# Wider recurrence operations, paired gate products, layer norm on ScalarE and a new order inside `y`, in a fused state-space and SwiGLU kernel

## The chip, the cores and the metric

The kernel runs on one core of one Trainium2 chip. The metric is the device time of one execution in microseconds (us). TensorE (PE) multiplies matrices into PSUM; VectorE (DVE), ScalarE (ACT) and GpSimd (POOL) do the rest; SyncE (SP) issues most DMAs. Each engine works through its own instructions in program order.

## The reference

Two branches read the same layer-normed input and are added to it. `x` is 2048 x 512, the state has 512 complex elements, F is 1792; everything is in bf16 outside.

```
xn = layernorm(x)                                   # over the 512 features, no weights
# branch A: diagonal complex state space model
dt = exp(log_dt); Lam_bar = exp(dt * Lam)
B_bar = ((Lam_bar - 1) / Lam)[:, None] * Bmat
Bu = einsum("bld,pd->blp", xn, B_bar)
for t in range(L): h = Lam_bar * h + Bu[:, t]       # complex
yA = 2 * real(einsum("blp,dp->bld", hseq, Cmat)) + xn * Dskip
# branch B: SwiGLU
yB = (silu(xn @ w1) * (xn @ w3)) @ w2
out = x + yA + yB
```

## The kernel before

The 2048 rows are cut into four blocks of 512 (`b`), each of four chunks of 128 (`cl`). Features, states and F are cut into tiles of 128: 4 feature tiles (`dt`), 4 state tiles (`pt`), 14 F tiles (`f`).

- **Layer norm.** `ln_first` does block 0: statistics and apply on VectorE, transposes on TensorE, copies of PSUM into `xnT` on ScalarE. `ln_tasks(b)` makes the tasks of the other blocks: `ln_stats` of a chunk on VectorE, `finish_stats` on POOL, `apply` on VectorE with a DMA transpose of `xn` into `xnT` on SP's queue.
- **Parameters.** `params` and `params_w` make from `log_dt` and `Lambda` the decay `rho`, the angle per step `turn` and the complex weight `w2c`, on 128 x 4 elements, mostly on POOL. `table_angles(pt)` makes the cosines and sines `tabe` of 512 steps (four VectorE operations, three sines on ScalarE), `table_q(pt)` multiplies them by `w2c` into `tabq`.
- **`glu(b)`.** For each `f` eight matmuls of 512 columns into two PSUM tiles `gu_ps` (of four), then `evac`: `Silu` of one and a copy of the other on ScalarE (`g16`, `u16`); `gate` multiplies them on VectorE into `hgT`.
- **`bu(b)`.** For each state tile the real and imaginary input, four matmuls each into `bu_ps`, copied by ScalarE into `u`.
- **The recurrence** (`ssm_tasks`). The rotation by the angle tables turns the complex recurrence into two real ones. Per state tile: `pre` rotates `u` (three VectorE operations on 128 x 1024), two `scan` of 512 steps with decay `rho`, `post` rotates back into `h` (three operations). The scan of block b starts from the last column of `h` of block b − 1.
- **`res_tasks(b)`.** `xn * Dskip + x`, two VectorE operations on 128 x 2048.
- **`y(b)`.** For each chunk 14 matmuls of `hgT` with `w2` and 8 of `h` with `ct_re` and `ct_im` into one PSUM tile `y_ps` (of two); `finish` adds the residual on VectorE and sends the chunk out by DMA on SP's queue.

The order of the work on VectorE is set by a queue of tasks, `Filler`: each task has a cost in us, and the code of `glu`, `bu` and `y` calls `bg.fill(budget)` after a group of matmuls. A fill issues tasks while half the cost of the next one is within the budget carried so far; `flush(key)` issues all up to the last one with that key. In `y` before the change:

```
            if cl == CPB - 1 and b == NBLK - 1:
                bg.fill(100.0)
            else:
                bg.fill(4.0)
            while len(pend) > 1:
                finish()
```

The order of the whole is glu(0), bu(0), glu(1), bu(1), y(0), glu(2), bu(2), y(1), bu(3), glu(3), y(2), y(3). DMA loads stand in SP's queue in the order written, `late_loads` (blocks 2 and 3 of `x`, `dskip_row`, `ct_re`, `ct_im`) as the last task of the first queue.

Of the kernel before, what the change touches and what calls it, by code (L numbers as in the profile page):

```python
# [21 lines left out]
class Filler:  # L22
# [8 lines left out]

    def fill(self, budget):
        self.debt += budget
        while self.tasks and self.tasks[0][0] * 0.5 <= self.debt:
            cost, fn, _ = self.tasks.popleft()
            self.debt -= cost
            fn()
        if not self.tasks:
            self.debt = min(self.debt, 0.0)

    def flush(self, key):
        last = -1
        for i, t in enumerate(self.tasks):
            if t[2] == key:
                last = i
# [8 lines left out]
def kernel(  # L54
# [133 lines left out]
    def ln_first():  # L188
        ln_alloc(0)
        for h in range(2):  # L190
            c0 = 2 * h
            for cl in (c0, c0 + 1):
                ln_stats(0, cl)
            lnv = lnp.tile([P, 2], FP32, name="lnv")
            nc.scalar.activation(out=lnv, in_=mv_all[:, c0:c0 + 2, 1], func=ACT.Ln, bias=eps_t, scale=1.0)
            nc.scalar.activation(out=rstd_all[:, c0:c0 + 2], in_=lnv, func=ACT.Exp, scale=-0.5)
            for cl in (c0, c0 + 1):
                ln_apply(0, cl)
                pxt = ps_y.tile([P, NDT, P], BF16, name="y_ps")
                for dt in range(NDT):  # L200
                    nc.tensor.transpose(out=pxt[:, dt, :], in_=xn_blk[0][:, cl, dt * P:(dt + 1) * P], identity=ident)  # L201
                nc.scalar.activation(out=xnT_blk[0][:, :, cl * P:(cl + 1) * P], in_=pxt, func=ACT.Copy)

    def ln_tasks(b):
# [100 lines left out]
    def bu(b):  # L305
        for pt in range(NPT):
            u = up.tile([P, 2, TBLK], BF16, name="u")
            for ri, bt in ((0, bt_re), (1, bt_im)):
                ps = ps_bu.tile([P, TBLK], FP32, name="bu_ps")
                for dt in range(NDT):  # L310
                    nc.tensor.matmul(out=ps, lhsT=bt[:, dt, pt * P:(pt + 1) * P], rhs=xnT_blk[b][:, dt, :],  # L311
# [211 lines left out]
```

## Time and profile before

| | |
|---|---|
| time, median of 3 runs | 236.75 us (236.69 to 237.62) |
| the profiled execution | 236.88 us, span 234.7 us |
| mean granted TensorE clock | 0.975 |
| TensorE matmuls busy | 210.3 us (90% of the span) |
| VectorE busy | 173.9 us (74%) |
| ScalarE busy | 97.1 us (41%) |

The span runs from the first to the last instruction of the profiled execution. Matmuls are pipelined and their ends are modelled, so TensorE's busy time is not time at its peak; the granted clock is 1.00 at 2.4 GHz.

### The profile page before, as it was taken

What the parts mean: (1) busy time and instruction counts of PE and PEld (TensorE: products, weight loads), DVE (VectorE), ACT (ScalarE), POOL (GpSimd) and SP (SyncE); (2) the same over time, 40 slices, a digit from 0 to 9 for tenths busy, and PEclk for the clock granted to TensorE, in tenths of its full rate; (3) what the DMA queues carried; (4) which work ended last, traced back from release to release, by engine and by line L of the source; (5) the groups of instructions that cost most, each with busy time, mean ns of one, the idle gap of its engine ahead of it and who ended that gap; (6) DMA issues with size and microseconds to landing.
All of it is one profiled execution on the core that took longest, in us unless ns stands there. A gap on an engine that the chain in (4) does not pass through costs nothing.

```text
span 234.7 us, 2666 instructions
## 1 busy us (share of the span) xinstructions
PE 210.3 (90%) x942; PEld 96.0 (41%) x961; DVE 173.9 (74%) x293; ACT 97.1 (41%) x171; POOL 14.5 (6%) x46
## 2 busy tenths in 40 slices
PE   0689989929999999599999999699999999999993
PEld 0454434314444444244444444244444444444441
DVE  2509799992989797996899599996999989711111
ACT  3459978614676630003676650002766670000000
POOL 6046002000000002000000100000000000000000
PEclk9999999997999999799999999889999999999998
DMA  6999500159300002201000031001000000100010
GB/s 191 353 303 253 199 3 0 22 128 216 106 0 0 0 3 45 67 22 45 0 3 3 0 67 22 25 22 45 0 0 3 0 0 0 46 24 22 22 45 24
DMA packets 25596, 13.66 MB, mean 58 GB/s; under 512 B 15472, under 2 KB 25584, under 8 KB 25584
## 3 DMA queue, kind: packets, MB, share of 16 engines
q1 hardware_dynamic: 25200, 13.24, 20.8%
q10 hardware_dynamic: 288, 0.26, 0.3%
q8 instruction: 7, 0.11, 0.2%
q14 instruction: 5, 0.04, 0.1%
q0 software_dynamic: 96, 0.00, 0.0%
HBM read 7.74 MB, written 2.10 MB: 42 GB/s over the span
## 4 chain that ended last, share of the span: by engine, by line
PE 62%; DVE 27%; ACT 2%; DMA 2%; issue 2%; POOL 2%; POOLq 0%; SPq 0%; ACTq 0%
PE gu_ps L363 33%; PE y_ps L428 17%; PE y_ps L431 9%; DVE g L335 4%; DVE stats L176 3%; PE bu_ps L311 3%; DVE hgT L375 2%; DVE xn L181 2%; DVE tabq L293 1%; DVE tabq L298 1%; DVE v L329 1%; DVE ang L282 1%; DMA x_blk<-in_A_x_dram 1%; DMA xnT<-xn 1%; DVE mv_all L177 1%
## 5 line engine op out<-in xcount | busy, mean ns | idle before, releaser
L363 PE MATMUL gu_ps<-xnT,w_sb 128*128 128x512 bf16 (+1 forms) x456 | 101.7, 383 | 6.8 <-DMA xnT<-xn 4.5
L363 PEld LDWEIGHTS <-w_sb 128*128 128x128 bf16 x464 | 46.6, 101 | 60.7 <-issue 10.1
L428 PE MATMUL y_ps<-w_sb,hgT 128*128 128x512 bf16 x219 | 53.9, 398 | 4.9 <-DVE o L421 4.6
L428 PEld LDWEIGHTS <-hgT 128*128 128x128 bf16 x224 | 22.7, 102 | 34.0 <-issue 9.7
L313 ACT ACTIVATE u<-bu_ps 128x512 bf16<-128x512 f32 x32 | 19.0, 597 | 31.1 <-PE bu_ps L311 31.1
L421 DVE TENSOR_TENSOR o<-y_ps,xn 128x512 bf16<-128x512 f32 x16 | 11.0, 685 | 27.5 <-PE y_ps L431 24.2
L335 DVE TENSOR_TENSOR_SCAN g<-rho,h,v 128x512 bf16<-128x512 f32 x24 | 30.0, 1274 | 0.2
L431 PEld LDWEIGHTS <-h 128*128 128x128 bf16 x128 | 12.5, 98 | 15.1
L311 PE MATMUL bu_ps<-xnT,bt_re 128*128 128x512 bf16 x62 | 16.2, 379 | 0.6 <-ACT u L313 0.5
L431 PE MATMUL y_ps<-ct_re,h 128*128 128x512 bf16 x63 | 16.4, 379 | 0.1
L311 PE MATMUL bu_ps<-xnT,bt_im 128*128 128x512 bf16 x62 | 16.3, 379 | 0.2
L431 PE MATMUL y_ps<-ct_im,h 128*128 128x512 bf16 x63 | 16.2, 379 | 0.0
L176 DVE BATCH_NORM_STATS2 stats<-x_blk 128x6 f32<-128x512 bf16 x16 | 10.8, 676 | 3.4 <-DMA x_blk<-in_A_x_dram 3.4
L368 ACT ACTIVATE g_1102<-gu_ps 128x512 bf16<-128x512 f32 x1 | 0.6, 598 | 23.7 <-PE gu_ps L363 23.7
L311 PEld LDWEIGHTS <-bt_re 128*128 128x128 bf16 x64 | 6.3, 98 | 8.3 <-issue 0.9
L335 DVE TENSOR_TENSOR_SCAN g<-rho,v 128x512 bf16<-128x512 f32 x8 | 9.5, 1212 | 0.0
L201 PE MATMUL y_ps<-ident,xn 128*128 128x128 bf16 x16 | 2.1, 308 | 8.2 <-DVE xn L181 8.2
L311 PEld LDWEIGHTS <-bt_im 128*128 128x128 bf16 x64 | 6.3, 98 | 7.5
L181 DVE TENSOR_SCALAR xn<-x_blk,mv_all,rstd_all 128x512 bf16<-128x512 bf16 x16 | 5.6, 408 | 4.2 <-POOL rstd_all L210 2.9
L209 POOL TENSOR_SCALAR vpe<-mv_all 128x4 f32<-128x4 f32 x3 | 0.8, 255 | 107.5 <-DVE mv_all L177 107.5
L260 DVE RECIPROCAL sc<-sc 128x4 f32<-128x4 f32 x1 | 0.2, 179 | 8.1 <-POOL sc L255 8.1
L201 PEld LDWEIGHTS <-xn 128*128 128x128 bf16 x16 | 1.5, 135 | 8.4 <-DVE xn L181 8.4
(331 smaller groups left out, 215.5 us busy)
## 6 DMA issues: line engine op xcount, KB each, us to landing
w_sb<-in_B_w_dram SPq DMA_DIRECT2D x6, 512.0 KB, 8.2
out_dram<-o SPq DMA_DIRECT2D x16, 128.0 KB, 1.7
w_sb<-in_B_w_dram SPq DMA_DIRECT2D x1, 1792.0 KB, 10.2
x_blk<-in_A_x_dram SPq DMA_DIRECT2D x3, 512.0 KB, 4.2
w_sb<-in_B_w_dram SPq DMA_DIRECT2D x2, 256.0 KB, 4.4
x_blk<-in_A_x_dram ACTq DMA_DIRECT2D x2, 128.0 KB, 3.0
x_blk<-in_A_x_dram SPq DMA_DIRECT2D x2, 128.0 KB, 2.7
xnT<-xn SPq DMA_TRANSPOSE x12, 2.4
```

Source lines behind the costliest of these rows:

```text
L176: nc.vector.bn_stats(out=stats, in_=x_blk[b][:, cl, :])
L177: nc.vector.bn_aggr(out=mv_all[:, b * CPB + cl, :], in_=stats)
L181: nc.vector.tensor_scalar(out=xn_blk[b][:, cl, :], in0=x_blk[b][:, cl, :], scalar1=mv_all[:, c, 0:1], scalar2=rstd_all[:, c:c + 1], op0=AL ...
L201: nc.tensor.transpose(out=pxt[:, dt, :], in_=xn_blk[0][:, cl, dt * P:(dt + 1) * P], identity=ident)
L311: nc.tensor.matmul(out=ps, lhsT=bt[:, dt, pt * P:(pt + 1) * P], rhs=xnT_blk[b][:, dt, :], start=(dt == 0), stop=(dt == NDT - 1))
L313: nc.scalar.activation(out=u[:, ri, :], in_=ps, func=ACT.Copy)
L335: nc.vector.tensor_tensor_scan(out=st["g", pt][:, ri, :], data0=rho[:, pt:pt + 1].to_broadcast([P, TBLK]), data1=st["v", pt][:, ri, :], in ...
L363: nc.tensor.matmul(out=ps[:, tsl], lhsT=w[:, dt, f * P:(f + 1) * P], rhs=xnT[:, dt, tsl], start=(dt == 0), stop=(dt == NDT - 1))
L375: nc.vector.tensor_tensor(out=hgT[:, f, :], in0=g16, in1=u16, op=ALU.mult)
L421: nc.vector.tensor_tensor(out=o, in0=y_ps, in1=xn_blk[b][:, cl, :], op=ALU.add)
L428: nc.tensor.matmul(out=y_ps, lhsT=hg_blk[b][:, f, tsl], rhs=w2_sb[:, f, :], start=(f == 0), stop=False)
L431: nc.tensor.matmul(out=y_ps, lhsT=h_blk[b][:, pt, ri, tsl], rhs=ct[:, pt, :], start=False, stop=(ri == 1 and pt == NPT - 1))
```

## The change

- Filler: only tidied (`pop`).
- Block 0's layer norm is split: `ln_first_pair` (statistics and apply of two chunks) and `ln_first_transpose`. The half-width matmuls of the first two `f` are issued after the first pair, and the second pair's transposes between the two halves. The transpose of the parameters stands ahead of the first matmuls, in a `bu_ps` tile; the table load for `Silu` stands after the last copy into `xnT`. The third `f` takes its PSUM from `ps_bu`.
- The first queue has a new order; `late_loads` is issued after `glu(0)`.
- `ln_scalar_engine(b)`, for blocks 2 and 3, replaces their tasks: sum by `Copy`, sum of squares by `Square`, apply by `Identity`, all on ScalarE, with the small steps on POOL. It is issued just ahead of `y(0)` and `y(1)`.
- The recurrence takes two state tiles in each operation (128 x 2048), and writes over its inputs: over `u` before and in the scans, over `h` after them. Its operations are tasks of their own.
- Gate products are made for two `f` at once (128 x 1024).
- `y` issues the gate part of two chunks, then the state part of each with its `finish`.
- Buffers: `glup` 3 to 2 (of double size), `up` 6 to 3 (of double size), `outp` 3 to 2.

```diff
-    glup = ctx.enter_context(tc.tile_pool(name="glup", bufs=3))
+    glup = ctx.enter_context(tc.tile_pool(name="glup", bufs=2))
...
-    up = ctx.enter_context(tc.tile_pool(name="up", bufs=6))
+    up = ctx.enter_context(tc.tile_pool(name="up", bufs=3))
...
+    def ln_scalar_engine(b):
+
+        ln_alloc(b)
+        acc = lnp.tile([P, 4, CPB], FP32, name="acc")
+        sm, nm, ss, nb = (acc[:, i, :] for i in range(4))
+        rstd = rstd_all[:, b * CPB:(b + 1) * CPB]
+        xn, gp = xn_blk[b], nc.gpsimd
+        for cl in range(CPB):
+            nc.scalar.activation(out=xn[:, cl, :], in_=x_blk[b][:, cl, :], func=ACT.Copy, accum_out=sm[:, cl:cl + 1])
+        gp.tensor_scalar(out=nm, in0=sm, scalar1=-1.0 / D, scalar2=None, op0=ALU.mult)
+        for cl in range(CPB):
+            nc.scalar.activation(out=xn[:, cl, :], in_=x_blk[b][:, cl, :], func=ACT.Square, bias=nm[:, cl:cl + 1],
+                                 scale=1.0, accum_out=ss[:, cl:cl + 1])
+        gp.tensor_scalar(out=ss, in0=ss, scalar1=1.0 / D, scalar2=LN_EPS, op0=ALU.mult, op1=ALU.add)
+        gp.tensor_tensor(out=rstd, in0=ss, in1=mhalf, op=ALU.pow)
+        gp.tensor_tensor(out=nb, in0=nm, in1=rstd, op=ALU.mult)
+        for cl in range(CPB):
+            nc.scalar.activation(out=xn[:, cl, :], in_=x_blk[b][:, cl, :], func=ACT.Identity,
+                                 bias=nb[:, cl:cl + 1], scale=rstd[:, cl:cl + 1])
+            ln_transpose(b, cl)
...
+    def params(pps, between):
         nc.scalar.activation(out=par, in_=pps, func=ACT.Copy)
         nc.scalar.activation(out=dtv, in_=par[:, 0:NPT], func=ACT.Exp)
         gp.tensor_tensor(out=kr, in0=dtv, in1=lre, op=ALU.mult)
+        between()
...
+        for hf in range(NPT // 2):
+            u = up.tile([P, 2, 2, TBLK], BF16, name="u")
+            u_blk[b, hf] = u
+            for j in range(2):
+                pt = 2 * hf + j
...
+            bg.fill(3.4)
...
+        FULL = [P, 2, 2, TBLK]
+
+        def half(hf):
+            psl = slice(2 * hf, 2 * hf + 2)
+            st = {}
+
+            def pre_a():
+                if hf == 0:
+                    h_blk[b] = hp.tile([P, NPT, 2, TBLK], BF16, name="h")
+                st["g"] = u_blk[b, hf]
+                st["p"] = ssmw.tile(FULL, BF16, name="p")
+                nc.vector.tensor_tensor(out=st["p"], in0=st["g"], in1=tabq[:, psl, 2:3, :].to_broadcast(FULL),
+                                        op=ALU.mult)
+
+            def pre_b():
+                nc.vector.tensor_tensor(out=st["g"], in0=st["g"], in1=tabq[:, psl, 0:2, :], op=ALU.mult)
+
+            def pre_c():
+                nc.vector.tensor_tensor(out=st["g"], in0=st["g"], in1=st["p"][:, :, ::-1, :], op=ALU.subtract)
+
+            def scan(j, ri):
+                pt = 2 * hf + j
+                init = 0.0 if b == 0 else h_blk[b - 1][:, pt, ri, TBLK - 1:TBLK]
+                v = st["g"][:, j, ri, :]
+                nc.vector.tensor_tensor_scan(out=v, data0=rho[:, pt:pt + 1].to_broadcast([P, TBLK]), data1=v,
+                                             initial=init, op0=ALU.mult, op1=ALU.add)
+
+            def post_a():
+                st["p"] = ssmw.tile(FULL, BF16, name="p")
+                nc.vector.tensor_tensor(out=st["p"], in0=st["g"], in1=tabe[:, psl, 1:3, :], op=ALU.mult)
+
+            def post_b():
+                nc.vector.tensor_tensor(out=h_blk[b][:, psl, :, :], in0=st["g"],
+                                        in1=tabe[:, psl, 0:1, :].to_broadcast(FULL), op=ALU.mult)
+
+            def post_c():
+                nc.vector.tensor_tensor(out=h_blk[b][:, psl, :, :], in0=h_blk[b][:, psl, :, :],
+                                        in1=st["p"][:, :, ::-1, :], op=ALU.subtract)
+
+            for fn in (pre_a, pre_b, pre_c):
+                bg.add(1.2, fn)
+            for j in range(2):
+                for ri in range(2):
+                    bg.add(1.25, lambda j=j, ri=ri: scan(j, ri))
+            for fn in (post_a, post_b, post_c):
+                bg.add(1.2, fn, ("ssm", b))
...
+            if f % 2 == 0:
+                pair[:] = [glup.tile([P, 2, TBLK], BF16, name="g16"), glup.tile([P, 2, TBLK], BF16, name="u16")]
+            g16, u16 = pair
+            nc.scalar.activation(out=g16[:, f % 2, :], in_=g_ps, func=ACT.Silu)
+            nc.scalar.activation(out=u16[:, f % 2, :], in_=u_ps, func=ACT.Copy)
+            if f % 2 == 1:
+                pend.append((f, g16, u16))
...
+                evs = [ln_first_transpose(2 * hf + i) for i in range(2)]
+                if hf == 0:
+                    pps = params_transpose()
+                    for ev in evs:
+                        ev()
+                    ln_first_pair(1)
+                else:
+                    params(pps, evs[0])
+                    evs[1]()
+                    nc.scalar.preload_act_table_set("silu_and_others")
...
+            bg.fill(4.0)
+            gate()
         for f in range(f0, NFT):
-            g_ps = ps_gu.tile([P, TBLK], FP32, name="gu_ps")
+            pool, name = (ps_bu, "bu_ps") if b == 0 and f == f0 else (ps_gu, "gu_ps")
+            g_ps = pool.tile([P, TBLK], FP32, name=name)
             mms(g_ps, w1_sb, f, slice(0, TBLK))
-            u_ps = ps_gu.tile([P, TBLK], FP32, name="gu_ps")
+            u_ps = pool.tile([P, TBLK], FP32, name=name)
             mms(u_ps, w3_sb, f, slice(0, TBLK))
             evac(f, g_ps, u_ps)
-            bg.fill(1.3)
-            while len(pend) > 1:
+            bg.fill(1.35)
+            if pend and f % 2 == 0:
...
+        tiles = {}
+
+        def from_gate(cl):
+            tiles[cl] = ps_y.tile([P, D], FP32, name="y_ps")
             for f in range(NFT):
-                nc.tensor.matmul(out=y_ps, lhsT=hg_blk[b][:, f, tsl], rhs=w2_sb[:, f, :], start=(f == 0), stop=False)
+                nc.tensor.matmul(out=tiles[cl], lhsT=hg_blk[b][:, f, cl * P:(cl + 1) * P], rhs=w2_sb[:, f, :],
+                                 start=(f == 0), stop=False)
+
+        def from_state(cl):
             for ri, ct in ((0, ct_re), (1, ct_im)):
                 for pt in range(NPT):
-                    nc.tensor.matmul(out=y_ps, lhsT=h_blk[b][:, pt, ri, tsl], rhs=ct[:, pt, :],
+                    nc.tensor.matmul(out=tiles[cl], lhsT=h_blk[b][:, pt, ri, cl * P:(cl + 1) * P], rhs=ct[:, pt, :],
                                      start=False, stop=(ri == 1 and pt == NPT - 1))
-            pend.append((cl, y_ps))
-            if cl == CPB - 1 and b == NBLK - 1:
-                bg.fill(100.0)
-            else:
-                bg.fill(4.0)
-            while len(pend) > 1:
-                finish()
-        return finish
-
-
-    ln_first()
-    ln1a, ln1b = ln_tasks(1)
+
+        def finish(cl):
+            o = outp.tile([P, D], BF16, name="o")
+            nc.vector.tensor_tensor(out=o, in0=tiles[cl], in1=xn_blk[b][:, cl, :], op=ALU.add)
+            nc.sync.dma_start(out=ov[:, b * CPB + cl, :], in_=o)
+
+        for cl in range(0, CPB, 2):
+            from_gate(cl)
+            bg.fill(2.8)
+            from_gate(cl + 1)
+            bg.fill(2.8)
+            if cl == 0:
+                bg.flush(("ssm", b))
+                bg.flush(("res", b))
+            from_state(cl)
+            finish(cl)
+            bg.fill(1.0)
+            from_state(cl + 1)
+            finish(cl + 1)
+            bg.fill(1.0)
...
+    bg.add(1.9, lambda: table_angles(0))
     bg.add(0.2, params_w)
-    for i in range(NPT + 1):
-        if i < NPT:
-            bg.add(1.9, lambda pt=i: table_angles(pt))
-        for t in ln1a[i:i + 1]:
-            bg.add(*t)
-        if i >= 1:
-            bg.add(2.1, lambda pt=i - 1: table_q(pt))
+    ln1a, ln1b = ln_tasks_vector(1)
+    for t in ln1a:
+        bg.add(*t)
+    bg.add(1.9, lambda: table_angles(1))
+    bg.add(2.4, lambda: table_q(0))
     for t in ln1b:
         bg.add(*t, ("ln", 1))
-    bg.add(0.0, late_loads)
+    for i in range(2, NPT):
+        bg.add(1.9, lambda pt=i: table_angles(pt))
+        bg.add(2.4, lambda pt=i - 1: table_q(pt))
+    bg.add(2.4, lambda: table_q(NPT - 1))
...
+    late_loads()
...
+    ln_scalar_engine(2)
+    y(0)
...
+    ln_scalar_engine(3)
+    y(1)
```

## Rows read from the trace of the kernel before

**Rows 1.** The page: busy time of engines, and ScalarE's in 40 slices (tenths).

```profile
PE 210.3 (90%) x942; PEld 96.0 (41%) x961; DVE 173.9 (74%) x293; ACT 97.1 (41%) x171; POOL 14.5 (6%) x46
...
ACT  3459978614676630003676650002766670000000
```

**Rows 2.** TensorE timeline: start, us, instruction and count, idle time before it.

```profile
10.03 3.62 PE L363 MATMUL gu_ps<-xnT,w_sb 128*128 128x256 bf16 x16
...
16.70 9.01 PE L363 MATMUL gu_ps<-xnT,w_sb 128*128 128x512 bf16 x39 [0.57 <-ACT g_259 L368]
...
45.91 1.03 PE L311 MATMUL bu_ps<-xnT,bt_im 128*128 128x512 bf16 x4
51.46 26.02 PE L363 MATMUL gu_ps<-xnT,w_sb 128*128 128x512 bf16 x110 [4.52 <-DMA xnT<-xn]
...
84.22 3.19 PE L428 MATMUL y_ps<-w_sb,hgT 128*128 128x512 bf16 x14
...
107.62 24.34 PE L363 MATMUL gu_ps<-xnT,w_sb 128*128 128x512 bf16 x110
131.79 1.03 PE L311 MATMUL bu_ps<-xnT,bt_re 128*128 128x512 bf16 x4
...
138.70 3.19 PE L428 MATMUL y_ps<-w_sb,hgT 128*128 128x512 bf16 x14
...
161.57 1.03 PE L311 MATMUL bu_ps<-xnT,bt_re 128*128 128x512 bf16 x4
...
192.69 3.18 PE L428 MATMUL y_ps<-w_sb,hgT 128*128 128x512 bf16 x14
...
229.89 1.03 PE L431 MATMUL y_ps<-ct_im,h 128*128 128x512 bf16 x4
```

**Rows 3.** Windows of 5 us: busy time of each engine, PEclk, DMA share, GB/s.

```profile
50.00:55.00 5.00, 3.54 (x11) 1.42 (x12) 2.59 (x5) 1.19 (x2) 0.00 (x0) 0.73 0.76 181
```

**Rows 4.** Waits: who waited for whom, us in total, times, longest.

```profile
PE y_ps L428 <- DVE o L421: 4.6, 2, 2.6
```

**Rows 5.** VectorE timeline.

```profile
17.57 0.18 DVE L260 RECIPROCAL sc<-sc 128x4 f32<-128x4 f32 x1 [8.10 <-POOL sc L255]
...
44.54 1.38 DVE L181 TENSOR_SCALAR xn<-x_blk,mv_all,rstd_all 128x512 bf16<-128x512 bf16 x4
...
95.72 0.67 DVE L421 TENSOR_TENSOR o<-y_ps,xn 128x512 bf16<-128x512 f32 x1
...
138.74 2.46 DVE L335 TENSOR_TENSOR_SCAN g<-rho,h,v 128x512 bf16<-128x512 f32 x2
...
145.22 2.46 DVE L335 TENSOR_TENSOR_SCAN g<-rho,h,v 128x512 bf16<-128x512 f32 x2
```

**Rows 6.** DMA issues: KB each, median us from issue to landing.

```profile
xnT<-xn SPq DMA_TRANSPOSE x12, 2.4
...
par_rows<-in_A_Lambda_im_dram POOLq DMA_DIRECT2D x1, 1.0 KB, 3.5
```

**Rows 7.** Groups by line: count, busy us, mean ns of one, idle before.

```profile
L335 DVE TENSOR_TENSOR_SCAN g<-rho,h,v 128x512 bf16<-128x512 f32 x24 | 30.0, 1274 | 0.2
...
L404 DVE TENSOR_TENSOR xn<-xn,dskip_row 128x2048 bf16<-128x2048 bf16 x4 | 4.9, 1218 | 0.0
L210 POOL TENSOR_TENSOR rstd_all<-vpe,mhalf 128x4 f32<-128x4 f32 x3 | 3.1, 1035 | 0.2
L293 DVE SCALAR_TENSOR_TENSOR tabq<-tabe,w2c,tq 128x512 bf16<-128x512 bf16 x4 | 3.0, 752 | 0.1
...
L285 ACT ACTIVATE tabe<-rnd,halfpi 128x512 bf16<-128x512 f32 x4 | 2.9, 722 | 2.0 <-DVE rnd L283 2.0
...
L243 ACT ACT_TABLE_LOAD x1 | 1.3, 1283 | 0.0
...
L325 DVE TENSOR_TENSOR p_599<-u,tabq 128x1024 bf16<-128x1024 bf16 x1 | 0.7, 685 | 0.0
```

**Rows 8.** ScalarE timeline at the front.

```profile
6.90 1.09 ACT L202 ACTIVATE xnT<-y_ps 128x512 bf16<-128x512 bf16 x2 [1.15 <-PE y_ps L201]
```

More of the change, by code (lines that the diff above doesn't have):

```diff
@@ L30, in add, with pop @@
         self.tasks.append((cost, fn, key))
+    def pop(self):
+        cost, fn, _ = self.tasks.popleft()
+        self.debt -= cost
+        fn()
     def fill(self, budget):
@@ L34, in fill @@
         while self.tasks and self.tasks[0][0] * 0.5 <= self.debt:
-            cost, fn, _ = self.tasks.popleft()
-            self.debt -= cost
-            fn()
+            self.pop()
         if not self.tasks:
@@ L41, in flush @@
     def flush(self, key):
[L42 to L45, printed above, removed]
+        last = max((i for i, t in enumerate(self.tasks) if t[2] == key), default=-1)
         for _ in range(last + 1):
-            cost, fn, _ = self.tasks.popleft()
-            self.debt -= cost
-            fn()
+            self.pop()
         self.debt = max(self.debt, -4.0)
@@ L186, in ln_alloc, with ln_first_pair, ln_first_transpose, ln_transpose @@
         xnT_blk[b] = xtp.tile([P, NDT, TBLK], BF16, name="xnT")
[L188 to L204, printed above, removed]
+    def ln_first_pair(h):
+        c0 = 2 * h
+        for cl in (c0, c0 + 1):
+            ln_stats(0, cl)
+        lnv = lnp.tile([P, 2], FP32, name="lnv")
+        nc.scalar.activation(out=lnv, in_=mv_all[:, c0:c0 + 2, 1], func=ACT.Ln, bias=eps_t, scale=1.0)
+        nc.scalar.activation(out=rstd_all[:, c0:c0 + 2], in_=lnv, func=ACT.Exp, scale=-0.5)
+        for cl in (c0, c0 + 1):
+            ln_apply(0, cl)
+    def ln_first_transpose(cl):
+        pxt = ps_y.tile([P, NDT, P], BF16, name="y_ps")
+        for dt in range(NDT):
+            nc.tensor.transpose(out=pxt[:, dt, :], in_=xn_blk[0][:, cl, dt * P:(dt + 1) * P], identity=ident)
+        return lambda: nc.scalar.activation(out=xnT_blk[0][:, :, cl * P:(cl + 1) * P], in_=pxt, func=ACT.Copy)
+    def ln_transpose(b, cl):
+        nc.sync.dma_start_transpose(out=xnT_blk[b][:, :, cl * P:(cl + 1) * P], in_=xn_blk[b][:, cl, :])
+    def ln_tasks_vector(b):
         csl = slice(b * CPB, (b + 1) * CPB)
@@ L305, in bu @@
     def bu(b):
[L306 to L311, printed above, removed]
-                                     start=(dt == 0), stop=(dt == NDT - 1))
-                nc.scalar.activation(out=u[:, ri, :], in_=ps, func=ACT.Copy)
-            u_blk[b, pt] = u
-            bg.fill(1.7)
@@ new lines, in bu @@
+        for hf in range(NPT // 2):
[3 more added lines that the diff above has]
+                pt = 2 * hf + j
+                for ri, bt in ((0, bt_re), (1, bt_im)):
+                    ps = ps_bu.tile([P, TBLK], FP32, name="bu_ps")
+                    for dt in range(NDT):
+                        nc.tensor.matmul(out=ps, lhsT=bt[:, dt, pt * P:(pt + 1) * P], rhs=xnT_blk[b][:, dt, :],
+                                         start=(dt == 0), stop=(dt == NDT - 1))
+                    nc.scalar.activation(out=u[:, j, ri, :], in_=ps, func=ACT.Copy)
+            bg.fill(3.4)
@@ new lines, in ssm_tasks @@
+    def ssm_tasks(b):
+        FULL = [P, 2, 2, TBLK]
[35 more added lines that the diff above has]
+                bg.add(1.2, fn, ("ssm", b))
+        for hf in range(NPT // 2):
+            half(hf)
```

89 lines of the change are left out of this document (15 added, 74 removed).

## The prediction

> **What bounds the kernel now.** I read the page first. TensorE (PE) is busy 90% of the span, VectorE (DVE) 74% [rows 1]. So the end is set by the matmuls, plus whatever keeps them from running back to back at the full clock.
>
> Next I read the TensorE timeline, which shows where that happens [rows 2]. Two stretches are clean. From 107.62 one `glu` takes until 131.79 (24.17 us, 1.73 a step of two tiles) and one `bu` until 138.70 (6.91 us), 31.08 together. The last two calls of `y` run from 192.69 to 229.89 + 1.03 = 230.92, 19.12 us each; a tile has 22 matmuls, so its 14 of the gate take 3.03 us and its 8 of the state 1.74. Against these, four stretches are too long.
> - Ahead of `glu(1)` TensorE stands still from 45.91 + 1.03 = 46.94 to 51.46 (4.52 us), waiting for the DMA transposes of block 1's layer norm. The `glu` and `bu` behind it take 84.22 − 51.46 = 32.76 us, 1.68 too many. The windows show why: 50 to 55 ran at a granted clock of 0.73 [rows 3], that is, partly at 1.2 GHz instead of 2.4 after the standstill. Two more windows, in `y(0)` and `y(1)`, look like it.
> - `y(0)` takes 107.62 − 84.22 = 23.40 us, 4.28 too many, and `y(1)` 161.57 − 138.70 = 22.87 us, 3.75 too many. The list of waits holds the cause: twice a tile of `y_ps` waits for `o` on VectorE, 2.6 us and 2.0 [rows 4]; the rest is again the slower clock after it.
> - The front: the half-width matmuls begin at 10.03, the full-width ones at 16.70 after waiting 0.57 us for ScalarE, and `bu(0)` ends at 46.94 [rows 2].
>
> All other time is matmuls at their pace, and 3.8 us from the last matmul to the end of the span.
>
> The VectorE timeline names what is late [rows 5]. Block 1's layer norm is applied only at 44.54, because the filler queue has all angle tables and `tabq` tables ahead of it. VectorE itself idled until 17.57, for the parameter chain on POOL. In `y(0)`, `finish` of tile 0 starts at 95.72, though its tile, the first of the four, was complete at 84.22 + 4.8 = 89.0: it stands behind queued recurrence work.
>
> **The change part by part.** I make the sum against the profiled execution, 236.88 us (span 234.7 and 2.18 around it); the median of the runs shown is 236.75.
>
> *Layer norm of block 1 earlier.* In the new queue its statistics follow `table_angles(0)` and its four applies follow `table_q(0)`. By the filler's bookkeeping (1.35 a step against the tasks' costs) the applies are issued in steps f = 6 and 7 of `glu(0)`, about 27 us into the span; a transpose lands 2.4 us after its issue [rows 6], so near 31. They are needed near 45. The standstill and its slow clock go: −4.52 − 1.68 = −6.2. `late_loads` still stands behind these transposes on SP's queue; its `ct_re` and `ct_im` are wanted only in `y(0)`, near 80.
>
> *The order inside `y`.* `from_gate` of two tiles comes first, then the state part of each, with its `finish` at once. The third tile needs the buffer that `finish` of tile 0 frees. That `finish` can start when the first state part is done, 2 × 3.03 + 1.74 = 7.8 us into `y`; TensorE asks for the buffer at 9.5. What counts is how much VectorE has queued ahead of that `finish`. For `y(0)`, counted from the start of `bu(1)`: the last gate product and three tasks, then from 5.4 on half of block 1's recurrence through its scans, to about 14.1; the state part ends at 6.9 + 7.8 = 14.7. No wait. For `y(1)`, counted from `bu(2)`: the recurrence can't start before the first pair of `u` is evacuated at 4.1, and a whole half (12.1 us, below) stands ahead of `finish`, which ends at 16.2 + 0.7 = 16.9; TensorE asks at 16.4. A wait of 0.5 us. For `y(2)`: tasks until 7.8, just in time. So −4.3 for `y(0)` and −3.75 + 0.5 = −3.2 for `y(1)`.
>
> *Recurrence two tiles wide, in place.* A row like the new operations exists: `xn` times the broadcast `dskip_row`, 2048 wide and written over its input, 1.22 us [rows 7]. So neither width, nor writing over an input, nor a broadcast costs the rate. A 1024-wide product takes 0.685. A state tile took 145.22 − 138.74 = 6.48 us from scans to scans [rows 5], two of them 12.96. A half block is now six wide operations and four scans; consecutive operations overlap by some 0.03 (two scans of 1.274 took 2.46 with what follows), so 6 × 1.2 + 4 × 1.23 = 12.1 us. The scan with its output over its input has no row: not less than the row of 1.274 [rows 7], for it does the same steps, and at most twice that; I take the row, for only an address differs. Gate products in pairs: by the slope of the two rows one of 512 takes 0.42, so 28 × (2 × 0.42 − 0.685) is some 4 us. So VectorE loses 8 × 0.86 = 7 and 4 us, and besides these the layer norm of blocks 2 and 3 (the applies alone 1.38 a block [rows 5]). The end sees none of it directly, since VectorE is not waited for outside the places above; it is the slack on which they rest. Were it to cost as much as before, `y(1)` would wait 0.7 us longer.
>
> *Layer norm of blocks 2 and 3 on ScalarE.* Per block twelve activations 512 wide, four small POOL operations (the power takes 1.04 [rows 7]) and four transposes. They start as `y` starts, where ScalarE has nothing else (the zeros in its slices [rows 1]). The forms that accumulate a sum have no row. Below: 0.5 us, from two copies in 1.09 [rows 8]; above: twice the sine with a bias, 0.72 [rows 7], in case a second instruction reads the sum. I take 0.75, as that sine too has an operand per partition: 12 × 0.75 + 2.2 (POOL) + 0.6 + 2.4 (last transpose) + 0.3 = 14.5 us, against the 19.1 of `y`. Cost 0; at the upper price it is 22.8, and the reader of `xnT` would wait 3.7. The Trainium skill, "ScalarE: Activation LUTs", section "What ACT_TABLE_LOAD costs", gives 186 ns plus 0.833 ns an element, 93 ns more for each per-partition operand, and 93 ns of overlap; by it the twelve would take an estimated 7.3 us instead of 9, and the sum would stay. No run here has timed these forms yet.
>
> *The front.* The first-half matmuls need only the first two chunks of `xnT`, ready at 6.90 + 1.09 = 7.99 [rows 8], not the 10.03 of before. `par_rows`, now read just ahead of them, lands 3.5 after an issue among the first of the span [rows 6], in time. Sixteen take 3.55, to 11.6; but now the second pair's transposes and ScalarE copies (about 1.0 each) stand between the halves, and the second half starts at 13.5, hardly earlier than it did. The table load (1.28) runs beside it, so the 0.57 wait goes: full-width matmuls from about 15.6, against 16.70. From there to the end of `bu(0)` the work is 12 × 1.73 + 6.91 = 27.7 us; before it took 46.94 − 16.70 = 30.2. Two waits stay. In step 3 VectorE has a gate product, two statistics and four angle operations to do, until about 21, and the three sines behind them hold up ScalarE's evacuations: about 1.0 us on TensorE. The last angle table does the same to `bu(0)`, 0.5. So `bu(0)` ends at 15.6 + 27.7 + 1.5 = 44.8: −2.1. Bounds: no gain (46.9), and no wait at all (15.3 + 27.7 = 43.0, −3.9).
>
> **Sum:** −6.2 − 4.3 − 3.2 − 2.1 = −15.8, so 236.88 − 15.8 = 221.1 us; the span near 219.
>
> **Rivals.**
> *A. `finish` is late again.* If each wide operation costs 0.15 us more than I take, the eight or nine ahead of `finish` make it 1.3 us later: `y(1)` waits 1.8, `y(0)` about 0.7. After waits of 2.0 and 2.6 the clock fell, and took another 1.7 each time. Price 2 to 7 us: 223 to 228. For it: margins of 0.6 and −0.5. Against: the row at 1.22.
> *B. ScalarE's layer norm is late.* At the upper price `glu(2)` and `bu(3)` each wait 3.7 and run 1.7 slower behind it: up to +11, 223 to 232. The skill's page named above, section "Table sets: the hidden batching unit", counts copy and identity into every set and does not name `Square`; if it needed two reloads, at the 1.28 us of the table load [rows 7], the 14.5 would be 17.1, still under 19.1.
> *C. The wide operations lose the packed rate,* for their third free dimension: the slower side. The nearest unpacked row is 0.752 for 512 elements [rows 7]; the two product rows give a fixed part of 0.15, so 2048 would take 4 × 0.60 + 0.15 = 2.55 us. From 47 us on VectorE has 97 (recurrence) + 10 (residual) + 13 (gates) + 8 (`finish`) to do, until 175; `y(3)` asks for the last state at 202. So 27 us more are hidden, and 27 + 16 = 43 more, 0.9 for each of the 48 wide operations, bring the kernel back to its old time. At +1.33 (64 us) it takes 221 + 37 = 258. Against: the broadcast row with two free dimensions keeps its rate, and the innermost step stays one element.
> *D. The waits only turn up elsewhere,* so that nothing moves: 235.7 to 238. Against it: four separate causes would each have to return.
>
> **How the numbers follow.** My forecast 0.70 (218 to 224, from the front's −3.9 to 0 and a `y(1)` wait of 0 to 1.5), A 0.13, B 0.08, C 0.05, D 0.04. Predicted: 221. The range, 217.5 to 228, holds the forecast, A and the cheaper half of B, some 0.85; it is not cut closer, because the front's clock is in no row. About 0.5% (1.2 us) is what a measurement of this kernel can tell from no change. Faster 0.91, same 0.03, slower 0.06.
>
> **What would show it.** No standstill between `bu(0)` and `glu(1)`, and a granted clock near 1.00 from 16 us to the end; each `y` in 19.1 to 19.7 us; `bu(0)` ending between 43 and 47; wide products at 1.2 us; ScalarE's layer norm done within 15 us of the start of `y`. It would be wrong if wide rows stood above 1.4 us, `y_ps` waited for `o` above 1 us, a matmul waited for `xnT`, or `bu(0)` ended after 47.

## The result, and the profile after

The changed kernel takes 220.53 us (median of 4 runs, 219.77 to 221.30) against 237.03 (236.69 to 237.62): a ratio of 0.930, 95% interval 0.926 to 0.934. Its profiled execution took 220.47 us, span 218.4. Other executions of the kernel before, that of the profile not among them, took near 233.4 us at a mean granted clock of 0.993 (near 237 it is 0.967 to 0.978), so some 3.5 us of the gain is clock that it loses in some executions only, and the ratios in the next section are to those within 1.5% of its fastest. The text below therefore compares places of profiled executions rather than ratios.

The page of the changed kernel, as in [rows 1], with the granted clock in 40 slices:

```profile
PE 203.8 (93%) x942; PEld 94.9 (43%) x961; DVE 158.7 (73%) x193; ACT 113.3 (52%) x211; POOL 19.5 (9%) x50
...
ACT  2378888776676775146676694216676630000000
...
PEclk9999999999999999999999999999999999999999
```

ScalarE's zeros under `y(0)` and `y(1)` are filled, and the clock is above 0.9 in every slice (0.998 in the mean). The window that stood at a clock of 0.73 [rows 3] is now:

```profile
50.00:55.00 5.00, 5.00 (x25) 2.29 (x24) 5.00 (x6) 3.46 (x7) 0.00 (x0) 1.00 0.02 3
```

TensorE's timeline, as in [rows 2]:

```profile
7.99 3.57 PE L405 MATMUL gu_ps<-xnT,w_sb 128*128 128x256 bf16 x16 [0.63 <-ACT xnT L200]
...
13.25 1.91 PE L405 MATMUL gu_ps<-xnT,w_sb 128*128 128x256 bf16 x16 [0.84 <-ACT xnT L200]
15.21 1.67 PE L405 MATMUL bu_ps<-xnT,w_sb 128*128 128x512 bf16 x7
...
23.29 13.97 PE L405 MATMUL gu_ps<-xnT,w_sb 128*128 128x512 bf16 x63 [1.23 <-ACT g_351 L414]
37.10 1.03 PE L339 MATMUL bu_ps<-xnT,bt_re 128*128 128x512 bf16 x4
...
44.17 24.34 PE L405 MATMUL gu_ps<-xnT,w_sb 128*128 128x512 bf16 x110
...
75.25 6.21 PE L476 MATMUL y_ps<-w_sb,hgT 128*128 128x512 bf16 x28
...
94.24 24.34 PE L405 MATMUL gu_ps<-xnT,w_sb 128*128 128x512 bf16 x110
118.41 1.03 PE L339 MATMUL bu_ps<-xnT,bt_re 128*128 128x512 bf16 x4
...
125.32 6.21 PE L476 MATMUL y_ps<-w_sb,hgT 128*128 128x512 bf16 x28
...
135.60 6.20 PE L476 MATMUL y_ps<-w_sb,hgT 128*128 128x512 bf16 x27 [0.62 <-DVE o L487]
...
145.09 1.03 PE L339 MATMUL bu_ps<-xnT,bt_re 128*128 128x512 bf16 x4
...
213.29 1.03 PE L482 MATMUL y_ps<-ct_im,h 128*128 128x512 bf16 x4
```

Set against [rows 2]: `bu(0)` ends at 44.17 instead of 46.94 (−2.77). `glu(1)` starts in the same moment, and until 75.25 it and `bu(1)` take 31.08 instead of 4.52 + 32.76 (−6.20). `y(0)` takes 18.99 instead of 23.40 (−4.41), `y(1)` 19.77 instead of 22.87 (−3.10). Together −16.5; the profiled executions differ by 236.88 − 220.47 = 16.4.

Of the waits, the two that [rows 4] corresponds to:

```profile
PE gu_ps L405 <- ACT g_351 L414: 1.2, 1, 1.2
PE y_ps L476 <- DVE o L487: 0.6, 1, 0.6
```

VectorE, as in [rows 5]:

```profile
9.86 0.49 DVE L304 TENSOR_SCALAR ang<-iota_f,turn 128x512 f32<-128x512 f32 x1 [0.44 <-POOL turn L270]
...
13.33 0.18 DVE L285 RECIPROCAL sc<-sc 128x4 f32<-128x4 f32 x1 [1.27 <-POOL sc L280]
...
26.05 0.73 DVE L179 TENSOR_SCALAR xn<-x_blk,mv_all,rstd_all 128x512 bf16<-128x512 bf16 x2
...
83.22 0.69 DVE L487 TENSOR_TENSOR o<-y_ps,xn 128x512 bf16<-128x512 f32 x1 [1.32 <-PE y_ps L482]
...
134.86 0.68 DVE L487 TENSOR_TENSOR o<-y_ps,xn 128x512 bf16<-128x512 f32 x1
```

The reciprocal that stood at 17.57 stands at 13.33, and block 1's last applies at 26.05 instead of 44.54. In `y(0)` VectorE waits for the first `finish`, not the other way round.

The wide recurrence operations by line (count, busy us, mean ns), as in [rows 7]:

```profile
L369 DVE TENSOR_TENSOR_SCAN u<-rho,h,u 128x512 bf16<-128x512 f32 x24 | 29.5, 1270 | 0.2
...
L360 DVE TENSOR_TENSOR u<-u,tabq 128x2048 bf16<-128x2048 bf16 x8 | 9.8, 1224 | 0.2
...
L356 DVE TENSOR_TENSOR p<-u,tabq 128x2048 bf16<-128x2048 bf16 x8 | 9.8, 1221 | 2.8 <-ACT u L341 2.8
```

The layer norm of block 2 under `y(0)`, in ScalarE's timeline:

```profile
75.94 0.62 ACT L231 ACTIVATE xn<-x_blk 128x512 bf16<-128x512 bf16 x1
76.46 0.19 ACT L231 ACTIVATION_READ_ACCUMULATOR xn<-x_blk 128x1 f32 x1
...
79.60 0.72 ACT L234 ACTIVATE xn<-x_blk,acc 128x512 bf16<-128x512 bf16 x1 [1.12 <-POOL acc L232]
...
85.13 2.93 ACT L240 ACTIVATE xn<-x_blk,acc,rstd_all 128x512 bf16<-128x512 bf16 x4 [2.60 <-POOL acc L238]
```

In POOL's timeline:

```profile
78.57 1.00 POOL L232 TENSOR_SCALAR acc<-acc 128x4 f32<-128x4 f32 x1 [54.16 <-ACT xn L231]
...
84.01 1.09 POOL L238 TENSOR_TENSOR acc<-acc,rstd_all 128x4 f32<-128x4 f32 x1
```

And on SP's queue:

```profile
85.97 5.13 SPq L203 DMA_TRANSPOSE xnT<-xn  x4
91.20 4.83 SPq L488 DMA_DIRECT2D out_dram<-o  x4
```

A sum costs a second instruction of 0.19 us. The four transposes take 5.13 us to issue, 1.28 each, so the last is issued at 89.8; with the 2.5 us to landing that the page of this profile gives as the median for this DMA it is there at an estimated 92.3. `glu(2)` asks at 94.24.

### The profile page after: what moved, and what is told of

It reads as the page before. It is cut to its first block, busy times and chain, and to the rows that moved or that the text cites. A ratio compares the mean times of both kernels' runs of the same rounds, so it can differ in the third digit from the quotient of the medians.

```text
span 218.4 us, 2557 instructions
## 1 busy us (share of the span) xinstructions
PE 203.8 (93%) x942; PEld 94.9 (43%) x961; DVE 158.7 (73%) x193; ACT 113.3 (52%) x211; POOL 19.5 (9%) x50
## 4 chain that ended last, share of the span: by engine, by line
PE 76%; DVE 11%; ACT 4%; DMA 4%; POOL 2%; issue 1%; SPq 1%; ACTq 0%; DVEq 0%
PE gu_ps L405 34%; PE y_ps L476 19%; PE y_ps L482 11%; PE bu_ps L339 11%; DMA ct_re<-in_A_C_re_dram 3%; DVE u L369 2%; DMA x_blk<-in_A_x_dram 1%; ACT xnT L200 1%; DVE xn L179 1%; DVE tabq L318 1%; DVE o L487 1%; DVE stats L174 1%; ACT L437 1%; DVE u L363 1%; DVE u L360 1%
## 5 line engine op out<-in xcount | busy, mean ns | idle before, releaser
L405 PE MATMUL gu_ps<-xnT,w_sb 128*128 128x512 bf16 (+1 forms) x449 | 97.4, 377 | 3.1 <-ACT xnT L200 1.5
L476 PE MATMUL y_ps<-w_sb,hgT 128*128 128x512 bf16 x220 | 49.3, 379 | 0.8 <-DVE o L487 0.6
L369 DVE TENSOR_TENSOR_SCAN u<-rho,h,u 128x512 bf16<-128x512 f32 x24 | 29.5, 1270 | 0.2
L482 PE MATMUL y_ps<-ct_re,h 128*128 128x512 bf16 x63 | 16.4, 379 | 0.2
L356 DVE TENSOR_TENSOR p<-u,tabq 128x2048 bf16<-128x2048 bf16 x8 | 9.8, 1221 | 2.8 <-ACT u L341 2.8
L360 DVE TENSOR_TENSOR u<-u,tabq 128x2048 bf16<-128x2048 bf16 x8 | 9.8, 1224 | 0.2
L363 DVE TENSOR_TENSOR u<-u,p 128x2048 bf16<-128x2048 bf16 x8 | 9.8, 1223 | 0.2
L381 DVE TENSOR_TENSOR h<-h,p 128x2048 bf16<-128x2048 bf16 x8 | 9.8, 1222 | 0.1
L374 DVE TENSOR_TENSOR p<-u,tabe 128x2048 bf16<-128x2048 bf16 x8 | 9.8, 1220 | 0.1
L377 DVE TENSOR_TENSOR h<-u,tabe 128x2048 bf16<-128x2048 bf16 x8 | 9.8, 1219 | 0.0
L369 DVE TENSOR_TENSOR_SCAN u<-rho,u 128x512 bf16<-128x512 f32 x8 | 9.3, 1210 | 0.1
```

The source lines that it names most:

```text
L356: nc.vector.tensor_tensor(out=st["p"], in0=st["g"], in1=tabq[:, psl, 2:3, :].to_broadcast(FULL), op=ALU.mult)
L360: nc.vector.tensor_tensor(out=st["g"], in0=st["g"], in1=tabq[:, psl, 0:2, :], op=ALU.mult)
L363: nc.vector.tensor_tensor(out=st["g"], in0=st["g"], in1=st["p"][:, :, ::-1, :], op=ALU.subtract)
L369: nc.vector.tensor_tensor_scan(out=v, data0=rho[:, pt:pt + 1].to_broadcast([P, TBLK]), data1=v, initial=init, op0=ALU.mult, op1=ALU.add)
L374: nc.vector.tensor_tensor(out=st["p"], in0=st["g"], in1=tabe[:, psl, 1:3, :], op=ALU.mult)
L377: nc.vector.tensor_tensor(out=h_blk[b][:, psl, :, :], in0=st["g"], in1=tabe[:, psl, 0:1, :].to_broadcast(FULL), op=ALU.mult)
```

## The experiments

The kernels start from the changed kernel unless it is said otherwise; 220.53 is the time to compare with.

**The order in `y`.** First it was undone (the code of `y` before, its `finish` called one tile late, and with it the fills of before: 8.0 us of budget ahead of the first `finish` instead of 5.6; the two were not taken apart):

```diff
-            from_gate(cl + 1)
...
+            pend.append((cl, y_ps))
+            bg.fill(4.0)
+            while len(pend) > 1:
+                finish()
```

> The changed kernel with the old order inside `y` (14 + 8 matmuls a tile, `finish` one tile later, a fill of 4.0 a tile), all else as changed. Theory (the place of `finish` in VectorE's queue removed the waits): in `y(1)` nine wide operations and four scans stand ahead of the first `finish`, which then ends at about 138.1 against 134.8 when TensorE asks: a wait of 3.3 and 1.7 of slow clock after it; in `y(0)` about 1 us in two waits. Total 220.5 + 0.3 + 0.8 + 5.0 - 0.8 = 225.8 us (224 to 228). Rival (the work taken off VectorE removed them, and the order adds nothing): 220.5 to 221.5 us, no wait of `y_ps` on `o` above 1 us.

225.23 us (225.06 to 226.45; ratio to before 0.963, 0.956 to 0.971). TensorE's timeline of this kernel, in `y(1)`:

```profile
138.88 1.44 PE L485 MATMUL y_ps<-w_sb,hgT 128*128 128x512 bf16 x3 [3.01 <-DVE o L478]
```

The window around it, of the same kernel:

```profile
138.00:142.00 4.00, 2.90 (x8) 1.16 (x9) 3.96 (x5) 0.85 (x2) 0.00 (x0) 0.57 0.55 101
```

The wait for `o` is back, and the clock falls behind it (0.57 in the window). Then the new `y` was put alone into the kernel before:

> The kernel before with the new order inside `y` alone. Theory (the place of `finish` sets the wait even with VectorE's old load): in `y(0)` VectorE reaches the first `finish` at about 93.3 and TensorE asks at 93.7, a wait of 0.4 at most; in `y(1)` it is there at 147.1 against 148.2, no wait. 237.0 - 4.3 - 3.75 + 0.4 = 229.3 us (228 to 231). Rival (with the old load the wait only moves): 235 to 237 us.

228.92 us (228.45 to 229.37; 0.970, 0.963 to 0.976), without any wait for `o`, with the standstill ahead of `glu(1)` unchanged at 4.5 us. So the order in `y` alone is worth 7.9 us by the medians (236.85 − 228.92), 5.0 between executions of nearly the same mean clock (233.54 at 0.993, 228.51 at 0.992), and 4.7 beside the rest. This kernel also has the old recurrence, the old gate products and the layer norm of blocks 2 and 3 on VectorE at once, so `y` loses its waits without any of the work that the change saves there.

**Queue and front.** The old first queue put back (angles, statistics and `tabq` tables mixed, `late_loads` as its last task):

> The changed kernel with the first queue in its old order (angle tables, statistics and `tabq` interleaved, the applies of block 1 and `late_loads` last). Theory (the place of the applies in the queue removed the standstill): VectorE is through with the tables at about 41.5, the last of the four transposes lands near 48.5, TensorE asks at 44.2: a wait of about 4.5 and 1.7 of slow clock, 226.5 us (224.5 to 228). Rival (VectorE's start 8 us earlier is enough): no standstill ahead of `glu(1)`, 220.5 to 221.5 us.

221.61 us (221.45 to 221.68; 0.947, 0.938 to 0.955). My theory missed by 5 us, and the rival was nearly right. VectorE's timeline of this kernel shows why, at block 1's applies:

```profile
38.44 1.38 DVE L179 TENSOR_SCALAR xn<-x_blk,mv_all,rstd_all 128x512 bf16<-128x512 bf16 x4
```

TensorE, at the start of `glu(1)`:

```profile
45.37 24.33 PE L405 MATMUL gu_ps<-xnT,w_sb 128*128 128x512 bf16 x110 [0.46 <-DMA xnT<-xn]
```

The applies are again behind all tables, but VectorE began them 5 us earlier (reciprocal at 12.55), so the transposes are only 0.46 us late. Next the front of the kernel before was put into the changed one: all four chunks ahead of the matmuls, parameters and table load between the half-width matmuls. One thing of the new front stays in: a fill of 4.0 ahead of the first gate product, which the kernel before doesn't have.

```diff
+                for i in range(2):
+                    ln_first_transpose(2 * h + i)()
...
+                if hf == 0:
+                    params(params_transpose(), lambda: None)
+                    nc.scalar.preload_act_table_set("silu_and_others")
```

> The changed kernel with the old front: all transposes of block 0 ahead of the first matmuls, the parameters and the table load between the halves; the first queue as changed. Theory (the front is worth what the traces show between 46.94 and 44.17): 2.7 us, 223.2 us (222 to 224.5), `bu(0)` ending near 47, the first angle table at 17.6, no standstill ahead of `glu(1)`. Rival (the tables and the pairs gave it, the order of the front nothing): 220.5 to 221 us.

225.36 us (224.56 to 225.63; 0.954, 0.948 to 0.959): 4.8 more, not 2.7. The first angle operation stands at 14.35 instead of 9.86. The sines of the second table, which stand ahead of the evacuations in ScalarE's order, wait for VectorE (2.65 us here, 0.65 in the changed kernel), and TensorE for them. ScalarE's timeline and TensorE's:

```profile
23.86 0.72 ACT L310 ACTIVATE tabe<-rnd,halfpi 128x512 bf16<-128x512 f32 x1 [2.65 <-DVE rnd L308]
...
26.16 15.43 PE L405 MATMUL gu_ps<-xnT,w_sb 128*128 128x512 bf16 x64 [3.50 <-ACT g L414]
```

So three more kernels separate the two edits: the changed kernel with both of them undone, and the kernel before with either of them alone.

> The change with the front and the first task queue of the kernel before together. With either one alone put back there was no standstill ahead of glu(1). My theory: the earlier start of VectorE and the new queue order each suffice to bring block 1's layer norm in time, and without both the standstill comes back: the tables end about 4 us later than in the run with the old queue alone (37.8), the applies come near 43, the last transpose lands near 49.5, TensorE asks near 48, so a wait of 1 to 2 us behind the 225.4 us of the old front, plus up to 1.7 of slower clock: 226.5 to 229 us. The rival: the queue order is worth nothing without the new front either: 225 to 225.8 us, no wait above 0.5 us at glu(1).

227.41 us (226.47 to 227.76; 0.973, 0.969 to 0.978). The number is as expected, its place is not: TensorE loses 5.07 us inside `glu(0)`, where the sines of two tables in a row hold up ScalarE, and so comes late enough to `glu(1)` to find the transposes there.

```profile
26.10 18.18 PE L405 MATMUL gu_ps<-xnT,w_sb 128*128 128x512 bf16 x71 [5.07 <-ACT g L414]
```

> The kernel before with the new order of the first task queue alone. My prediction put -4.5 us and up to -1.7 us of clock on this edit. My theory now: the standstill ahead of glu(1) goes, but VectorE starts late and the statistics now stand near the sines, so a step of glu(0) waits for ScalarE as in the run with the old front (up to 3.5 us), and part is given back: 231 to 234 us. A first rival: the whole term is real: 230.6 us. A second: no gain, 236 to 237.5 us.

232.16 us (229.69 to 232.97; 0.994, 0.990 to 0.998). By the medians this is 236.71 − 232.16 = 4.6 less; between executions of the same mean clock it is 3.4 at 0.993 (233.06 and 229.69) and 4.5 at 0.978 (236.71 and 232.26). In the profiled execution, the one of 229.69, the standstill is gone, and the wait that gives part of it back is in `bu(0)`, not in `glu(0)`:

```profile
43.35 1.02 PE L311 MATMUL bu_ps<-xnT,bt_re 128*128 128x512 bf16 x4 [2.21 <-ACT u L313]
...
46.80 24.34 PE L363 MATMUL gu_ps<-xnT,w_sb 128*128 128x512 bf16 x110
```

> The kernel before with the new front alone (split layer norm of block 0, parameters' transpose ahead of the matmuls, table load behind the last copy into xnT; gate products come in pairs with it, because the front's code uses them); old queue, old recurrence, old y, layer norm of blocks 2 and 3 on VectorE. My theory: the front is worth its own 2.7 to 4.3 us, and starting VectorE 6 us earlier shortens the standstill ahead of glu(1) from 4.5 to about 1 us: 228 to 231 us. The rival: only the 2.1 us that the prediction gave to the front, with the standstill as before: 234 to 235 us.

225.15 us (225.13 to 226.76; 0.966, 0.962 to 0.971), below both expectations: by the medians the front alone brings 11.6 us, and 7.9 against the executions of the kernel before at a mean clock of 0.993 (233.06). VectorE's timeline:

```profile
12.45 0.18 DVE L285 RECIPROCAL sc<-sc 128x4 f32<-128x4 f32 x1 [2.99 <-POOL sc L280]
...
38.35 1.38 DVE L179 TENSOR_SCALAR xn<-x_blk,mv_all,rstd_all 128x512 bf16<-128x512 bf16 x4
```

It starts 5.1 us earlier than in [rows 5], and the applies, still behind all tables, come 6.2 us earlier. TensorE's timeline, at `glu(1)` and in `y(0)`:

```profile
45.27 24.33 PE L388 MATMUL gu_ps<-xnT,w_sb 128*128 128x512 bf16 x110 [0.45 <-DMA xnT<-xn]
...
88.48 3.18 PE L468 MATMUL y_ps<-w_sb,hgT 128*128 128x512 bf16 x14 [2.47 <-DVE o L461]
```

The window of 5 us with the second of these waits:

```profile
86.00:91.00 5.00, 2.53 (x13) 1.17 (x12) 4.96 (x7) 0.00 (x0) 0.00 (x0) 1.00 0.07 26
```

`bu(0)` ends 2.1 us earlier, the standstill shrinks from 4.52 to 0.45, and the 1.7 of slow clock behind it goes: 7.9. The other 3.6 are in `y(0)` (21.62 instead of 23.40) and `y(1)` (21.06 instead of 22.87), where VectorE is still waited for (2.47 and 1.63) but the clock stays at 1.00, so that 14 matmuls after the wait take 3.18 instead of 4.87. That the front is what kept the clock up there isn't shown.

**Layer norm of blocks 2 and 3.** Put back to VectorE's queue (`ln_tasks_vector(2)` ahead of `y(0)`, `ln_tasks_vector(3)` behind it):

> The changed kernel with the layer norm of blocks 2 and 3 on VectorE, as tasks of the queue in their old places; nothing of it on ScalarE. Theory (VectorE has slack, and the end sees none of the 9 us): 220.0 to 221.5 us, waits of `y_ps` on `o` below 1.5 us in all. Rival (the move is a term of the gain): VectorE is late by the 5 us a block that it gets back, and `y(0)` or `y(1)` wait 2 to 4 us longer and run slower behind it: 223.5 to 228 us.

220.73 us (219.61 to 221.21; 0.942, 0.937 to 0.948): nothing, as expected. To find the margin on ScalarE, its first pass was made three times (eight copies more):

```diff
-        for cl in range(CPB):
+        for cl in list(range(CPB)) * 3:
```

> The changed kernel with ScalarE's first pass of blocks 2 and 3 (the copies with a sum) done three times: 8 more copies a block, 8 x 0.62 = 5.0 us, same result. Theory from the trace of the changed kernel (the last transpose lands near 92.4 with `glu(2)` at 94.2, and near 142.9 with `bu(3)` at 145.1, so margins of 1.9 and 2.2): waits of 3.1 and 2.8 and 1.7 of slow clock behind each, 229.8 us (227 to 232). Rival (the prediction's margin of 4.6): 0.4 each, 220.5 to 222 us.

224.94 us (224.01 to 225.42; 0.952, 0.946 to 0.959), between the two expectations. Of the difference, 0.9 stands already at the start of `y(0)` in the profiled execution (76.19 instead of 75.25), from the half-width matmuls (last section). TensorE waits at `glu(2)` and at `bu(3)`:

```profile
97.55 24.33 PE L405 MATMUL gu_ps<-xnT,w_sb 128*128 128x512 bf16 x112 [2.20 <-DMA xnT<-xn]
...
149.13 1.02 PE L339 MATMUL bu_ps<-xnT,bt_re 128*128 128x512 bf16 x4 [0.58 <-DMA xnT<-xn]
```

The copies take 8 x 0.61 = 4.9 us more, but the first POOL step is quicker (0.25 instead of 1.00), so the `Identity` pass starts at 90.22, 4.0 later against TensorE, which asks at 95.35 instead of 94.24. The margin is thus 4.0 − 2.2 = 1.8 us in `y(0)`; by the transposes (142.65 instead of 135.87, asked for 3.5 later) it is 3.3 − 0.6 = 2.7 in `y(1)`, and not the 4.6 that the prediction left for both. My theory added a slow clock behind the 2.2; the clock stayed at 1.00 there.

**The width.** The recurrence of the kernel before (one state tile, 128 x 1024, not in place; `up` with six buffers):

> The changed kernel with the recurrence one state tile wide and with tiles of its own for `v` and `g`, as before; angle scratch shares their tiles as before. Theory (the width gives VectorE 7 us of slack, of which the end sees only what stands ahead of the first `finish` of `y(1)`): the wait there grows from 0.6 to about 1.3 at most, 220.5 to 221.8 us. Rival (the 7 us are a term of the gain): 224 us or more.

219.71 us (219.56 to 220.37; 0.939, 0.934 to 0.944): below the expected range, and by medians 0.8 less than the changed kernel, though within its spread. VectorE's timeline in `bu(2)` and `y(1)`, first of the changed kernel, then of this one:

```profile
122.70 1.23 DVE L356 TENSOR_TENSOR p<-u,tabq 128x2048 bf16<-128x2048 bf16 x1 [2.76 <-ACT u L341]
```

```profile
121.05 0.69 DVE L350 TENSOR_TENSOR p<-u,tabq 128x1024 bf16<-128x1024 bf16 x1 [1.03 <-ACT u L338]
...
134.01 0.69 DVE L470 TENSOR_TENSOR o<-y_ps,xn 128x512 bf16<-128x512 f32 x1
135.10 0.69 DVE L470 TENSOR_TENSOR o<-y_ps,xn 128x512 bf16<-128x512 f32 x1 [0.40 <-PE y_ps L465]
```

In spite of more busy time (163.6 us against 158.7) the first `finish` comes 8.6 us after the start of `y(1)` (125.40), not 9.5 (134.86 − 125.32), and the wait of 0.62 is gone. In both kernels the same work stands ahead of it, the recurrence of two state tiles. It takes longer in the narrow form (134.01 − 121.05 = 12.96 us against 134.86 − 122.70 = 12.16), but it starts earlier: a narrow operation needs `u` of one state tile and starts 2.6 us after the start of `bu(2)` (118.49), while a wide one waits for `u` of two and starts 4.3 after it (118.41). Each gate product as two operations of 512:

```diff
-            nc.vector.tensor_tensor(out=hgT[:, f - 1:f + 1, :], in0=g16, in1=u16, op=ALU.mult)
+            for i in range(2):
+                nc.vector.tensor_tensor(out=hgT[:, f - 1 + i, :], in0=g16[:, i, :], in1=u16[:, i, :], op=ALU.mult)
```

> The change with each gate product of two f tiles issued as two operations 512 wide instead of one 1024 wide. My theory: the pair saves VectorE about 4 us in all, but only slack, so the time stays: 220.0 to 221.2 us. The rival: the added 0.15 us per product stands ahead of the recurrence and of `finish` and makes y(1) wait for `o` more than 0.6 us, or holds up the gate's buffers: 222 us or more.

220.10 us (219.96 to 221.53; 0.944, 0.941 to 0.947): slack, as expected.

**Both waits that are left.** One fill of `y(1)` moved behind its first `finish`, and the sines of an angle table issued behind the next evacuation:

```diff
-            bg.fill(2.8)
+            hold = 2.8 if b == 1 and cl == 0 else 0.0
+            bg.fill(2.8 - hold)
...
-            bg.fill(1.0)
+            bg.fill(1.0 + hold)
...
+        later.append(sines)
...
+            while later:
+                later.popleft()()
```

> The changed kernel with its two remaining waits attacked. In `y(1)` the fill ahead of the first `finish` is 0 and the 2.8 come after it; the three sines of an angle table stand on ScalarE behind the next evacuation and not ahead of it. Theory: the wait of 0.62 in `y(1)` goes, and of the 1.23 in step 6 of `glu(0)` some 1.0: 220.5 - 0.7 - 1.0 = 218.8 us (218 to 219.7). Rival (other waits take their place, since ScalarE is full in `glu(0)`): 219.7 to 221 us.

219.16 us (218.74 to 219.23; 0.928, 0.923 to 0.933), the fastest of all. The wait of 1.23 in `glu(0)` is gone, 0.40 stands in `bu(0)` in its place, and in `y(1)`:

```profile
137.25 3.18 PE L484 MATMUL y_ps<-w_sb,hgT 128*128 128x512 bf16 x14 [0.16 <-DVE o L495]
```

## Why the prediction was right, and where it was not

The time was 220.5 against 221, in the range, and the terms came out near their sizes place by place; but one term was put down to one edit where a second brings it as well.

- **The standstill, −6.2 by the queue order.** The size is right (−6.20), and the order suffices for it: with the new queue alone `y(0)` starts at 77.88 instead of 84.22, −6.3. But it isn't what it hangs on. The start of `y(0)` in the kernels with the edits apart:

| | old front | new front |
|---|---|---|
| kernel before, old queue | 84.22 | 76.35 |
| kernel before, new queue | 77.88 | not run |
| rest changed, old queue | 82.11 | 76.44 |
| rest changed, new queue | 79.58 | 75.25 |

In the two lower rows the old front still has the fill of 4.0 ahead of the first gate product. With the new front the queue is worth 1.2 us. The step that failed is the one on the front. I had read that VectorE idles until 17.57 for the parameter chain [rows 5], and gave the front only what it moves on TensorE, 0 to 3.9. Its larger effect is that everything queued on VectorE starts some 5 us earlier, and a standstill of 4.52 was all that was late. By the prediction's terms the change without the new queue would have taken some 6 us more and without the new front 2.1 more; the runs showed 1.1 (221.61) and, with that fill left in, 4.8 (225.36). That the sum held is luck in this term, for the two effects overlap and a wait can be removed only once: measured at their places in the profiled executions, the front alone saves 7.9 up to `y(0)`, the queue alone 6.3 and `y` alone 8.0 in its first two calls (19.24 and 18.99), together 22.2, against 16.4 for the whole change.
- **The front, −2.1.** At the end of `bu(0)` −2.77 here, −2.1 in the kernel with the front alone. Full-width matmuls from 15.21 (15.6 predicted); the waits 1.23 (1.0) and 0.16 (0.5). The sign "a matmul waited for `xnT`" was written too widely: the half-width matmuls of block 0 waited 0.63 and 0.84 for it, as the start of the second half at 13.5 (13.25) already implied.
- **The order inside `y`.** `y(0)` −4.41 (−4.28), its `finish` 14.9 us after the start of `bu(1)` (14.7). `y(1)` −3.10 (−3.2), its wait 0.62 (0.5). Undoing it alone and doing it alone both moved the time as expected. What I took as fixed, 1.7 of slow clock behind each wait, isn't: without it the term of the waits alone is 2.6 + 2.0 − 0.6.
- **Wide and in place.** 1.22 for the wide operations (1.2), 1.270 for the scan in place (1.274). They bring no time. The prediction said that the slack they gain shortens the wait in `y(1)` by 0.7. That reckoned the narrow form's cost from the wide form's start. The narrow form needs `u` of one state tile only, so it starts 1.7 us earlier, takes 0.8 longer, and has no wait there at all.
- **Layer norm on ScalarE, 14.5 us.** Some 16.4 from 75.94 to the estimated 92.3, so it was not done within 15 us of the start of `y`, as the prediction's signs had it. The activations were too dear (Copy 4 x 0.61, Square 4 x 0.71, Identity 2.93: 8.2, not 9), the two POOL stretches too cheap (1.12 + 2.60, not 2.2), and the transposes stand at 1.28 us each on SP's queue, so 4.2 us lie behind the last activation instead of 3.3. The estimate by the Trainium skill, "ScalarE: Activation LUTs", section "What ACT_TABLE_LOAD costs", was 7.3; the trace has eight reads of the accumulator on top, which set the copies 0.61 apart, where two without them took 1.09 together [rows 8]. What its section "Table sets: the hidden batching unit" leaves open of `Square` the trace settles: both table loads stand at the front, and none is near `y(0)`.
- **The rivals.** A stayed at 0.62, as forecast. B had 1.8 us of room left at `glu(2)`. C and D didn't come.

Why the old front costs 3.5 to 5.1 us inside `glu(0)` beside the rest of the change, but only 1.0 in the kernel before with the new queue, stands in ScalarE's timelines. Counted in evacuated `f`, the sines of the second angle table stand behind 7 with the new queue alone, behind 4 in the changed kernel with the old front, and behind 2 with the old front and queue: the fill of 4.0 puts them that early, and a VectorE that starts late makes ScalarE wait there.

What stays open: why the clock fell behind some waits and not behind others (below), and which part of the front starts VectorE earlier, since they were moved together only.

## What to carry to other kernels

If two edits can each remove the same wait, a sum of terms can come out right and the credit wrong; set the start of one place on the bound engine in a table of both edits. When an engine that is not the bound starts late, follow what is queued on it to the wait that this ends in, before an order is blamed. An operation over two tiles waits for the second of them: where a short task on the path stands behind it, the later start can cost more than the width saves.
